# Two early loads of a retention-plus-MLP kernel, each issued as 120 + 8 partitions

## The chip, the cores and the metric

The kernel runs on one core of a Trainium2 chip. The metric is the device time of one launch in microseconds (us), as the median of three runs. One further execution was profiled; its span (first to last instruction) and its own device time are given below beside that median.

## The reference, cut to what matters

Two stages follow each other, all in fp32 in the reference. First a linear attention with decay in blocks of 64 rows, for 4 batches x 8 heads, 768 rows, head dimension 64. Then a two-layer MLP over all 3072 rows, 512 wide, 2048 hidden:

```python
intra = np.einsum('bhic,bhjc->bhij', qb, kb) * Dmask[None]
intra = np.einsum('bhij,bhjd->bhid', intra, vb)
inter = np.einsum('bhid,bhde->bhie', qb * lam_pow[None], kv_state)
out[:, :, sl] = intra + inter
kv_state = lam_block * kv_state + np.einsum('bhsd,bhse->bhde', kb_dec, vb)
...
h = x @ w_in
g = 0.5 * h * (1.0 + np.tanh(c * (h + 0.044715 * h * h * h)))
return (g @ w_out)
```

## The kernel before, in words

The attention is cut into 24 steps. A step is 256 rows of one batch and four of the eight heads; it loads q, k and v as tiles of 128 partitions, each partition with four heads x two neighbouring rows x 64 numbers (256 KB for each of the three). Two steps together give the attention output of 256 rows, transposed into `xT`, which is the input of the MLP. The MLP's rows are worked off in seven groups; group 0 holds the first 512 rows, so the output of steps 0 to 3. `queue_group` puts a group's work, in small pieces, into the list `filler`, and `fill(n)` takes the next n pieces out of it. The main part of the kernel, from line 930 on, is an order written out by hand: `prep` (casts), `stage_t` (transposes), `R`/`products`/`causal`/`update` (attention) and `fill` in between. Every instruction is pinned, so each engine runs its instructions in the order of the program, and what stands behind a waiting instruction waits too.

The first weights `moe_w_in` come as four blocks of 512 columns, j = 0 to 3, into fp32 staging tiles of 128 partitions x 4 chunks x 512, and are cast to fp16 on the chip. Blocks 0 and 1 come in two parts, of two chunks each (512 KB); blocks 2 and 3 in one piece (1 MB). The second weights `moe_w_out` come as four loads of 1 MB into the same staging tiles. All these loads are issued on SP, in this order: q, k and v of steps 0 to 2 (v of step 0 on ACT), q and k of step 3, the first part of block 0, v of step 3, the second part of block 0, the two parts of block 1, blocks 2 and 3, the four loads of `moe_w_out`, then q, k and v of steps 4 to 8. `lam`, the decay of each head, is an 8-partition load on ACT at the very start.

The loads that the change touches, and who reads them:

- v of step 3 is read by `scale_v(3)` on GpSimd (line 266). On TensorE, `products(3, None, banks)` (line 385) reads its result, behind `fill(8)`, the first eight pieces of group 0 (line 838, which use the first part of block 0).
- the second part of block 0 is read by the casts `cast_win(0, 0, 256, 128, c23, on_act=True)` on ACT (line 108) and `cast_win(0, 256, 512, 256, c23)` on VectorE (line 110). The next pieces, `fill(4)` (line 838), need them.

Later places that the prediction speaks of: block 2 of the first weights is cast at line 110 and first read by the matmuls of line 561. After `fill(9)` the order goes on with `prep(4); stage_t(4); prep(5); ... stage_t(5)`: q of steps 4 and 5 is scaled on VectorE (line 282), k of step 4 cast on VectorE (line 293) and k of step 5 on ACT (line 295), and `stage_t` transposes both on TensorE (line 321).

Of the kernel before, what the change touches and what calls it, by code (L numbers as in the profile page):

```python
# [15 lines left out]
def kernel(  # L16
# [10 lines left out]
    nc = tc.nc  # L27
    pin = tc.keep_in_program_order
    P = 128
# [25 lines left out]
    ps_M = ctx.enter_context(tc.tile_pool(name="psM", bufs=8, space=PSUM))  # L55


    ld32 = {}

    def load_step(s, names="qkv"):  # L60
        b, r = divmod(s, 2 * NSB)
        sb, half = divmod(r, 2)
        ts = ld32.setdefault(s, [])
        for nm, src in (("q", q), ("k", k), ("v", v)):
            if nm not in names:
                continue
            t = ld.tile([P, HH, 2, D], FP32, tag=nm + "32", name=f"{nm}32_{s}")
            rows = src[b, half * HH : (half + 1) * HH, sb * SB : (sb + 1) * SB, :]
            queue = nc.scalar if (nm, s) == ("v", 0) else nc.sync
            pin(queue.dma_start(out=t[:].rearrange("p h j d -> p h (j d)"),  # L70
                                in_=rows.rearrange("h (p j) d -> p h (j d)", j=2)))
            ts.append(t)

    w_in16 = w16p.tile([P, NC, DFF], FP16)
# [13 lines left out]
    def load_win(j, part=None):  # L88
        if not part:
            wstage[("i", j)] = wst.tile([P, NC, 512], FP32, tag=f"w{j}", name=f"wi32_{j}")  # L90
        t = wstage[("i", j)]
        src = moe_w_in[:, j * 512 : (j + 1) * 512].rearrange("(c p) f -> p c f", p=P)
        cs = slice(0, NC) if part is None else slice(2 * part, 2 * part + 2)
        pin(nc.sync.dma_start(out=t[:, cs, :], in_=src[:, cs, :]))

    def load_wout(j):
        t = wst.tile([P, 4, DM], FP32, tag=f"w{(0, 2, 1, 3)[j]}", name=f"wo32_{j}")
# [58 lines left out]
    for s in range(3):  # L156
        load_step(s)
    load_step(3, "qk")
    load_win(0, 0)
    load_step(3, "v")  # L160
    load_win(0, 1)
    for j in range(1, 4):
        for part in ((0, 1) if j < 2 else (None,)):
            load_win(j, part)
# [996 lines left out]
```

## Time and profile before

| | |
|---|---|
| median of 3 runs | 198.84 us (198.81 to 199.01) |
| the profiled execution | 198.79 us, span 197.0 us, so 1.8 us lie around the span |
| granted TensorE clock | 1.000 |
| TensorE matmuls busy | 191.2 us of the span |
| VectorE, ScalarE, GpSimd busy | 149.0, 121.1, 74.4 us |
| loaded from HBM, stored to it | 27.26 MB, 6.29 MB |
| first-weight loads of 512 KB, issue to landing (median) | 7.1 us |
| v loads of 256 KB, issue to landing (median) | 5.2 us |

In the views below a line of the timeline gives start and duration in us, the engine, the line of the kernel, the operation, output<-input, shape and count; brackets give the idle time of that engine just before and what ended it. PE is TensorE's matmuls, PEld its weight loads, DVE VectorE, ACT ScalarE, POOL GpSimd, and SPq the queue of SyncE that issues loads. In the chain of waits a line is start, duration and what held the end of the program back at that time.

### The profile page before, as it was taken

Reading aid. Unit: us, or ns where it says so; the run is one execution under the profiler, and the core shown is the slowest. Engines: PE = TensorE matmul, PEld = TensorE weight load, DVE = VectorE, ACT = ScalarE, POOL = GpSimd, SP = SyncE. Lnnn points to the kernel's source line nnn. Section 1 sums busy time; section 2 is a strip of 40 time slices with the busy share of each in tenths; the row PEclk is TensorE's granted clock in tenths of the full one; section 3 lists DMA queues with packets and bytes.
Section 4 is the critical chain, followed back from the end, with each engine's and each line's share of the span. In section 5 each row is a group of like instructions: output and inputs, shape, how many; then the busy total and the mean of one; then the engine's idle time right before and its main releaser. Section 6 shows DMA issues by size and latency. Waiting matters only on the chain.

```text
span 197.0 us, 5913 instructions
## 1 busy us (share of the span) xinstructions
PE 191.2 (97%) x2431; PEld 140.1 (71%) x2431; DVE 149.0 (76%) x291; ACT 121.1 (61%) x249; POOL 74.4 (38%) x85
## 2 busy tenths in 40 slices
PE   8979999999999999999999999999999999999993
PEld 2556544446888888654688764578888888888882
DVE  4797722889999889859999927999656987487620
ACT  3663878357874685686845378844867746679221
POOL 6594213457554931169754517165002030002000
PEclk9999999999999999999999999999999999999999
DMA  5999999999999999999996998400211300020205
GB/s 167 292 324 384 387 383 386 300 285 297 259 220 248 257 333 231 213 238 288 226 294 132 274 310 202 92 7 0 53 67 42 107 6 2 0 110 29 77 19 198
DMA packets 62810, 38.13 MB, mean 194 GB/s; under 512 B 18624, under 2 KB 55744, under 8 KB 62784
## 3 DMA queue, kind: packets, MB, share of 16 engines
q1 hardware_dynamic: 62240, 37.50, 74.3%
q8 instruction: 19, 0.31, 0.7%
q10 hardware_dynamic: 544, 0.26, 0.5%
q14 instruction: 7, 0.06, 0.1%
HBM read 27.26 MB, written 6.29 MB: 170 GB/s over the span
## 4 chain that ended last, share of the span: by engine, by line
PE 89%; SPq 4%; DMA 4%; ACT 0%; issue 0%
PE Hps L561 25%; PE MX L640 18%; PE MY L640 9%; PE HX L739 7%; PE O2ps L576 7%; PE MW L640 4%; DMA wi<-in_moe_w_in_dram 4%; SPq L70 4%; PE HY L739 4%; PE S L350 3%; PE Hps L838 3%; PE HW L739 2%; PE OK L408 2%; PE O L461 1%; PE O L436 1%; PE OK L399 1%
## 5 line engine op out<-in xcount | busy, mean ns | idle before, releaser
L561 PE MATMUL Hps<-xT,w_in 128*128 128x512 f16 (+1 forms) x288 | 50.5, 332 | 0.0
L513 POOL TENSOR_TENSOR u<-t,lumask 128x256 f16<-128x256 f32 x40 | 30.9, 788 | 40.7 <-DVE t L506 27.0
L561 PEld LDWEIGHTS <-w_in 128*128 128x128 f16 x288 | 27.9, 98 | 19.1
L565 ACT ACTIVATE gT<-Hps 128x512 f16<-128x512 f32 x56 | 33.5, 598 | 11.6 <-PE Hps L561 11.1
L360 DVE TENSOR_TENSOR PT<-S,mask 128x512 f16<-128x512 f32 x48 | 30.3, 680 | 7.8 <-PE S L350 7.8
L266 POOL TENSOR_TENSOR v<-v,dv 128x512 f16<-128x512 f32 x24 | 28.7, 1197 | 15.2 <-DMA v<-in_v_dram 14.0
L640 PEld LDWEIGHTS <-gs 128*128 128x128 f16 x320 | 31.2, 98 | 3.6
L640 PEld LDWEIGHTS <-gT 128*128 128x128 f16 x240 | 23.3, 98 | 3.2 <-ACT gT L565 0.2
L640 PE MATMUL MX<-w_sum,gs 128*128 128x256 f16 x160 | 21.4, 273 | 0.0
L692 POOL TENSOR_TENSOR o<-u,q 128x512 f32<-128x512 f32 (+1 forms) x5 | 6.3, 1252 | 36.7 <-ACT u L657 36.7
L282 DVE TENSOR_TENSOR qk<-q,dq 128x512 f16<-128x512 f32 x23 | 19.1, 833 | 0.8 <-DMA q<-in_q_dram 0.7
L295 ACT ACTIVATE qk<-k 128x512 f16<-128x512 f32 x23 | 14.4, 625 | 7.4 <-DMA k<-in_k_dram 7.3
L610 DVE TENSOR_TENSOR gs<-gT 128x1024 f16<-128x1024 f16 (+1 forms) x24 | 16.9, 711 | 1.6 <-ACT gT L565 1.6
L576 PE MATMUL O2ps<-w_out,gT 128*128 128x512 f16 x64 | 14.6, 379 | 0.0
L487 ACT ACTIVATE xT<-OK 128x256 f16<-128x256 f32 x26 | 9.9, 452 | 7.0 <-PE OK L408 6.5
L739 PEld LDWEIGHTS <-ws 128*128 128x128 f16 x128 | 12.5, 98 | 1.6 <-issue 0.2
L487 ACT ACTIVATE xT<-O 128x256 f16<-128x256 f32 x22 | 8.0, 461 | 5.8 <-PE O L461 4.9
L657 ACT ACTIVATE u<-MX 128x256 f32<-128x256 f32 x18 | 6.9, 384 | 7.4 <-PE MX L640 7.3
L576 PEld LDWEIGHTS <-gT 128*128 128x128 f16 x64 | 6.1, 98 | 6.6
L350 PEld LDWEIGHTS <-qkT 64*64 64x64 f16 x384 | 6.0, 106 | 6.8 <-issue 3.6
L640 PE MATMUL MY<-w_out,gs 128*128 128x256 f16 x80 | 10.7, 273 | 0.0
L753 DVE COPY u<-HX 128x512 f32<-128x512 f32 x8 | 5.5, 688 | 6.8 <-ACT gT L757 4.3
(98 smaller groups left out, 318.4 us busy)
## 6 DMA issues: line engine op xcount, KB each, us to landing
q<-in_q_dram SPq DMA_DIRECT2D x24, 256.0 KB, 4.9
k<-in_k_dram SPq DMA_DIRECT2D x24, 256.0 KB, 5.0
v<-in_v_dram SPq DMA_DIRECT2D x23, 256.0 KB, 5.2
out_dram<-o SPq DMA_DIRECT2D x23, 256.0 KB, 4.3
wo<-in_moe_w_out_dram SPq DMA_DIRECT2D x4, 1024.0 KB, 9.4
wi<-in_moe_w_in_dram SPq DMA_DIRECT2D x4, 512.0 KB, 7.1
wi<-in_moe_w_in_dram SPq DMA_DIRECT2D x2, 1024.0 KB, 12.5
v<-in_v_dram ACTq DMA_DIRECT2D x1, 256.0 KB, 4.3
```

What stands on the lines that cost most here:

```text
L266: pin(nc.gpsimd.tensor_tensor(wide(tv[:]), ld32[s][2][:], decay(dv, s), ALU.mult))
L282: pin(q_eng.tensor_tensor(wide(tq), q32[:], decay(dq, s), ALU.mult))
L295: pin(nc.scalar.activation(out=wide(tk), in_=k32[:], func=AF.Copy))
L360: pin(nc.vector.tensor_tensor(t[:, hl].rearrange("p b c d -> p b (c d)"), Sps[:].rearrange("p b c d -> p b (c d)"), mask[:].unsqueeze(1).t ...
L487: pin(nc.scalar.activation(out=d, in_=o, func=AF.Copy))
L513: pin(nc.gpsimd.tensor_tensor(u[:], state[half][:].unsqueeze(2).to_broadcast([P, 2, 2, D]), lumask[:, 2 * half : 2 * half + 2, :].unsqueez ...
L561: pin(nc.tensor.matmul(by_block(Hps[:, i, :]), w_in16[:, c, f * P : (f + 1) * P], x(c), start=(c == 0), stop=(c == NC - 1)))
L565: pin(nc.scalar.activation(out=dst, in_=Hps[:], func=AF.Gelu_apprx_tanh))
L576: pin(nc.tensor.matmul(O2[tau][0][:], gT[:, f % HF, f // HF, tau * P : (tau + 1) * P], w_out16[:, f, :], start=(n == 0), stop=(n == NF - 1)))
L610: pin(nc.vector.tensor_tensor(g_rows(m, i), g_rows(a, i), g_rows(b, i), op))
L640: pin(nc.tensor.matmul(dst, lhsT, rhs, start=(opens and i == 0), stop=(closes and i == HF - 1), skip_group_check=True))
L739: pin(nc.tensor.matmul(dst[:, i, :], w_in_block(a, slice(c, c + 1), slice(f * P, f * P + P))[:, 0], x_block(b, slice(c, c + 1))[:, 0], sta ...
```

## The change

The v load of step 3 and the load of the second part of block 0 are each issued as two transfers on SP: one of partitions 0 to 119 and one of partitions 120 to 127. The bytes, the tiles, the order of all loads and every reader stay. A reader now waits for two transfers. All other loads stay single.

```diff
+    even, uneven = (slice(0, P),), (slice(0, 120), slice(120, P))
     ld32 = {}
 
     def load_step(s, names="qkv"):
...
             queue = nc.scalar if (nm, s) == ("v", 0) else nc.sync
-            pin(queue.dma_start(out=t[:].rearrange("p h j d -> p h (j d)"),
-                                in_=rows.rearrange("h (p j) d -> p h (j d)", j=2)))
+            for ps in uneven if (nm, s) == ("v", 3) else even:
+                pin(queue.dma_start(out=t[ps].rearrange("p h j d -> p h (j d)"),
+                                    in_=rows.rearrange("h (p j) d -> p h (j d)", j=2)[ps]))
             ts.append(t)
...
         cs = slice(0, NC) if part is None else slice(2 * part, 2 * part + 2)
-        pin(nc.sync.dma_start(out=t[:, cs, :], in_=src[:, cs, :]))
+        for ps in uneven if (j, part) == (0, 1) else even:
+            pin(nc.sync.dma_start(out=t[ps, cs, :], in_=src[ps, cs, :]))
```

## The prediction

> **What bounds the kernel now.** I read the page first: which engine carries the time, whether the DMA queues are full, and how the chain that ended last is made up.
>
> ```profile
> PE 191.2 (97%) x2431; PEld 140.1 (71%) x2431; DVE 149.0 (76%) x291; ACT 121.1 (61%) x249; POOL 74.4 (38%) x85
> ...
> DMA  5999999999999999999996998400211300020205
> ...
> PE 89%; SPq 4%; DMA 4%; ACT 0%; issue 0%
> ```
>
> TensorE bounds the kernel, but each digit of the DMA row is 4.9 us, so up to about 100 us the 16 DMA queues are full as well. Both loads of the change lie in that time. The chain of waits from 0 to 35 us says where DMA holds the end:
>
> ```profile
> 9.35 0.47 SPq L70
> 9.81 0.04 issue
> 9.86 7.88 DMA wi<-in_moe_w_in_dram
> 17.74 0.02 issue
> 17.77 0.42 ACT w_in L108
> 18.19 0.05 issue
> 18.24 1.13 PE Hps L838 x8
> ```
>
> The load on this chain is the second part of block 0, issued at 9.86 and landed at 17.74. Everything behind it is TensorE. So I asked the timeline how long TensorE waits for it, and the DMA view of 13.5 to 15.5 us why it lands so late.
>
> ```profile
> 16.47 1.04 POOL L266 TENSOR_TENSOR v<-v,dv 128x512 f16<-128x512 f32 x1 [1.51 <-DMA v<-in_v_dram]
> ...
> 18.23 0.11 PEld L838 LDWEIGHTS <-w_in 128*128 128x128 f16 x2 [0.45 <-ACT w_in L108]
> 18.24 1.13 PE L838 MATMUL Hps<-xT,w_in 128*128 128x256 f16 x8 [0.35 <-ACT w_in L108]
> ...
> 18.54 0.55 PEld L838 LDWEIGHTS <-w_in 128*128 128x128 f16 x6 [0.19 <-ACT w_in L108]
> ```
>
> ```profile
> q8 instruction: 1, 0.02, 3.7%
> ```
>
> One instruction fetch of 16 KB sits between the loads there. The packet record has it at 13.81 us, 1.17 us long. The landing records hold one arrival for each queue of a transfer. The first part of block 0, before the fetch, has arrivals from 13.84 to 14.13 and the last at 14.32. For v of step 3 fifteen came by 15.11 and the sixteenth at 16.40; for the second part of block 0, by 16.46 and at 17.74. So one queue lost 1.3 us to the fetch and both readers wait for it. A second fetch starts at 20.08 (1.05 us), and block 2 has two late arrivals, 23.10 and 23.12, against 21.83 for the fourteenth: it fell on another queue. Call the first late queue X and the second Y.
>
> Last I asked what stands between 18 us and the end:
>
> ```profile
> 37.73 0.92 DVE L282 TENSOR_TENSOR qk<-q,dq 128x512 f16<-128x512 f32 x1 [0.53 <-DMA q<-in_q_dram]
> 38.64 0.43 DVE L293 CAST qk<-k 128x512 f16<-128x512 f32 x1
> 38.71 0.65 PEld L321 LDWEIGHTS <-qk 128*128 128x128 f16 x8
> ...
> 41.40 0.63 ACT L295 ACTIVATE qk<-k 128x512 f16<-128x512 f32 x1 [3.51 <-DMA k<-in_k_dram]
> ...
> 42.08 0.23 PEld L321 LDWEIGHTS <-qk 128*128 128x128 f16 x4 [0.20 <-ACT qk L295]
> ```
>
> This is the view that decides. The transposes of step 4 start 0.06 us after VectorE has scaled q, which waited for a load. Those of step 5 wait 0.20 us for ScalarE, which had waited 3.51 us for k of step 5 (landed at 41.32; the arrivals 41.29 and 41.32 I take for X and Y, the others came by 41.02). So at 42.08 TensorE is held by DMA again; in the waits from 43 to 110 us only GpSimd still waits for loads (9.4 us, three times), and the matmul row has no gap there.
>
> **The change part by part.** *What it removes.* 128 partitions give 16 arrivals, and `lam`, the one 8-partition load, gives eight; 120 does not divide by 16 but does by 15. I take 15 queues with 8 partitions each for the large transfer, 8 queues with one each for the small. Then one queue carries nothing of the two loads, eight carry 9 partitions and seven carry 8. If the idle queue is X, v lands near 15.1 and the weights near 16.5, each up to 0.35 later by what follows. TensorE then finds the cast done: 0.35 (matmul gap) + 0.19 (the weight load's second wait) = 0.54 us saved at 18.2 to 18.6. The other weight-load gap of 0.21 at 17.57 also stands at 19.30 with no wait behind it, so it is not counted. Nothing in the trace says which queue has the fetch; if X is another one, this saving is nothing.
>
> *What it adds on the queues.* Full transfers follow each other in 0.90 us for v (landings 0.90 apart) and 1.35 for a half block (17.74 to 19.10). One partition of eight more is 0.11 + 0.17 = 0.28 us on eight queues. Each extra transfer also costs a fixed bit: 32 packets of 27 ns are 0.86 of the 0.90, so about 0.04, twice: 0.07. Sum 0.35 us. These queues stay full beyond the loads of step 5, so this delay is carried on to each of them. It can't be below 0.28 if the split is 9 to 8. The readers' wait is now for the later of two landings, the small transfer's, since it stands behind the large one on the eight queues. Behind the waiting scale of v on GpSimd stand the u products of line 513, behind the cast on ScalarE the copies into xT (line 487), and TensorE waits for both; these 0.35 us are the price already counted, not a second one.
>
> *What it adds on SP.* Two more issues of 0.47 us (the rows of 10.68 to 11.70), 0.94 in all. Behind them on SP stand block 1's parts, blocks 2 and 3, then `moe_w_out`. The weights' second part is issued at 9.86, but its packets can't start before v's are through at about 15; the last of the row, block 3, is issued by 13.2 and starts after 21.5. The lead hides it: 0. Without it, up to 0.94.
>
> *Where the saving goes.* 0.54 us of lead at 18.6 reaches line 561 at 24.03, where block 2's first cast (23.14 + 0.43) leaves 0.46 of room: nearly all survives. At 38.71 it ends: q of step 4 lands at 37.71 whatever TensorE did, because Y is as late as X (37.70 and 37.71). At 42.08 it ends once more. So with X relieved the net is 41.32 - 41.29 = 0.03 us saved if Y is one of the seven, and 0.35 lost if Y is one of the eight, since q of step 4 and k of step 5 then land 0.35 later, and VectorE, ScalarE and TensorE wait for them in order. With X not relieved, it is 0.35 lost if X or Y is one of the eight. Eight of fifteen queues make the first chance 0.53; two draws out of fifteen make the second 1 - (7/15)(6/14) = 0.80. Most of the weight lies on +0.35: 198.79 + 0.35 = 199.14 for the profiled execution, and its median stands 0.05 higher: 199.2.
>
> [...]
>
> **The rivals.** *The 120-partition transfers run below full rate* (slower). No row shows a part transfer of any size. The mechanism is fewer queues or a shared path into the tile: were the large one to run on 8 queues, as `lam` does, each would carry 16 partitions instead of 8, so 0.90 + 1.35 = 2.25 us more. That lands on k of step 5 in full: 201.1. Half of that gives 200.0. It decides from 0.05 us over the 0.35 on. For it: 120 is no multiple of 16. Against it: queues work off packets one by one, 2 KB in 84 to 95 ns, which looks like each queue's own limit. [...]
>
> *The saving at 18.2 stays* (faster): 198.84 - 0.54 = 198.3. For it: this is the only gap in the matmul row after 13.3 us. Against it: 42.08, where k of step 5 would have to land 0.3 us earlier, with Y still late.
>
> *Nothing moves:* Y, and X if it is not relieved, are among the seven: 198.8.
>
> **How the numbers follow.** About 0.2% (0.4 us) is what a measurement of this kernel can tell from no change. Forecast, eight queues set the pace: chance 0.47, price 0.28 to 0.6 (the fixed bit may be larger than 0.04), so 0.29 within the line and 0.18 beyond it. Rate lost: 0.30, all slower. Nothing moves: 0.13. Saving stays: 0.10, faster. That is faster 0.10, same 0.42, slower 0.48. The range 198.6 to 200.4 holds the forecast (alone 199.1 to 199.5), the unmoved case and two thirds of the rate case; it leaves out the saving and the far end of the rate case, 0.2 together.
>
> **What would show it.** Right: the weight load's 0.45 and 0.19 at 18.2 are gone or not, as X is relieved or not; the wait of 0.20 at line 321 before k of step 5 grows to 0.5 or more with k landing near 41.65; after it the timeline is that of before, shifted. Rate lost: the fifteen early arrivals of v and of the weights move beyond 15.5 and 17.2. Wrong altogether: k of step 5 lands before 41.0 and the end moves up with it.

## The result, and the profile after

The changed kernel takes 202.02 us (median of 4 runs, 201.18 to 202.5) against 198.84 before: a ratio of 1.015, with an interval from 1.013 to 1.017. (Here and below a ratio is worked out from all runs of both kernels, so it can differ a little from the quotient of the two medians.) The forecast was 199.2 and its range ended at 200.4. The profiled execution took 202.5 us, span 200.7, at a mean granted clock of 0.991; before it was 198.79, 197.0 and 1.000. The page of after, read as the page of before was:

```profile
PE 192.4 (96%) x2431; PEld 140.9 (70%) x2431; DVE 150.2 (75%) x291; ACT 121.3 (60%) x249; POOL 74.3 (37%) x85
...
PEclk9999699999999999999999999999999999999999
DMA  6999999999989999999998999320202200021114
...
PE 88%; DMA 5%; SPq 4%; ACT 0%; issue 0%; ACTq 0%
```

TensorE is busy for 192.4 us instead of 191.2, with the same 2431 matmuls, and the clock row has a 6 in its fifth slice (20 to 25 us). DMA's share of the chain has grown from 4% to 5%. The DMA row shows next to nothing: the queues look as full as before. The chain of waits from the same stretch:

```profile
9.83 0.45 SPq L73
10.27 0.04 issue
10.32 9.44 DMA wi<-in_moe_w_in_dram
19.79 0.05 issue
19.84 0.43 ACT w_in L112
20.27 0.04 issue
20.31 1.89 PE Hps L842 x8
```

Two things differ. The load is 9.44 us on its way instead of 7.88 and is issued 0.46 us later, behind the second transfer of v; and the eight matmuls behind it take 1.89 us instead of 1.13. The windows (start:end and length, then each engine's busy time, and at the end granted clock, DMA share, GB/s) of the changed kernel show what lies behind both:

```profile
14.50:18.10 3.60, 3.20 (x52) 2.20 (x53) 2.64 (x8) 1.33 (x4) 1.07 (x2) 1.00 1.07 213
...
20.20:23.60 3.40, 3.29 (x30) 2.01 (x31) 1.96 (x5) 0.83 (x4) 1.36 (x2) 0.50 1.05 384
23.60:28.00 4.40, 4.40 (x26) 2.42 (x25) 3.02 (x8) 3.67 (x8) 0.73 (x1) 1.00 1.04 383
```

and the kernel before, for the stretch in which the same two loads move:

```profile
14.50:16.20 1.70, 1.70 (x43) 1.24 (x42) 1.70 (x8) 1.46 (x4) 0.46 (x1) 1.00 1.04 373
```

The share of busy queue time is 1.0 in both, but the queues move 213 GB/s in place of 373. The packet records say how: a packet of 2 KB takes 84 to 85 ns (median) in the second part of block 0 before, and 159 ns in the changed one. So here a full DMA row was no sign of a full rate. After 20.2 us, when only transfers of 128 partitions are left, the rate is 384 GB/s again. The second finding stands in the same lines: from 20.20 to 23.60 TensorE was granted 0.50 of its clock.

The timeline of the changed kernel around the two waits:

```profile
17.38 1.04 POOL L270 TENSOR_TENSOR v<-v,dv 128x512 f16<-128x512 f32 x1 [2.53 <-DMA v<-in_v_dram]
...
18.47 0.32 PE L389 MATMUL OK<-v,qk 64*64 64x64 f16 x16 [0.55 <-POOL v L270]
...
19.84 0.72 ACT L112 ACTIVATE w_in<-wi 128x256 f16<-128x256 f32 x2 [3.85 <-DMA wi<-in_moe_w_in_dram]
...
20.31 1.04 PE L842 MATMUL Hps<-xT,w_in 128*128 128x256 f16 x4 [1.52 <-ACT w_in L112]
```

A gap of 0.35 us before has become gaps of 0.55 and 1.52, after one of 0.22 at 16.66. The landing records, of the same two loads and of what follows (us):

| arrivals | before | after, large transfer | after, small transfer |
|---|---|---|---|
| v of step 3 | 14.69 to 15.11, last 16.40 | 15.08 to 15.91, last 17.31 | 15.39 to 15.99 |
| second part of block 0 | 16.05 to 16.46, last 17.74 | 17.66 to 18.15, last 19.75 | last 18.71 |
| block 1, last of each part | 19.10, 20.45 | 20.85, 22.21 | |
| q of step 4, k of step 5 | 37.71, 41.32 | 39.59, 43.19 | |

The loads behind are 1.75 to 2.0 us late, all of them up to step 5. But TensorE is later still. Its landmarks (us): the matmuls that wait for the weights start at 18.24 before and 20.31 after (+2.07); those of block 2 at 24.25 and 27.68 (+3.43, so 1.36 more in the stretch at half clock); the transposes of step 4 at 38.92 and 42.36; the last matmul ends at 193.72 and 196.95 (+3.23); the span ends 3.29 us after that before, and 3.77 after (+0.48). Those last two make the 3.71 us of the two spans.

### The profile page after: what moved, and what is told of

It is laid out like the page before. It is cut to its first block, busy times and chain, and to the rows that moved or that the text cites. A ratio compares the mean times of both kernels' runs of the same rounds, so it can differ in the third digit from the quotient of the medians.

```text
span 200.7 us, 5919 instructions
## 1 busy us (share of the span) xinstructions
PE 192.4 (96%) x2431; PEld 140.9 (70%) x2431; DVE 150.2 (75%) x291; ACT 121.3 (60%) x249; POOL 74.3 (37%) x85
## 4 chain that ended last, share of the span: by engine, by line
PE 88%; DMA 5%; SPq 4%; ACT 0%; issue 0%; ACTq 0%
PE Hps L565 24%; PE MX L644 17%; PE MY L644 9%; PE HX L743 7%; PE O2ps L580 7%; DMA wi<-in_moe_w_in_dram 5%; PE MW L644 4%; SPq L73 4%; PE HY L743 3%; PE Hps L842 3%; PE S L354 3%; PE HW L743 2%; PE OK L412 2%; PE OK L403 1%; PE O L465 1%; PE O L440 1%
## 5 line engine op out<-in xcount | busy, mean ns | idle before, releaser
L517 POOL TENSOR_TENSOR u<-t,lumask 128x256 f16<-128x256 f32 x40 | 31.4, 799 | 44.6 <-DVE t L510 30.5
L696 POOL TENSOR_TENSOR o<-u,q 128x512 f32<-128x512 f32 (+1 forms) x5 | 5.7, 1145 | 36.6 <-ACT u L661 36.6
```

The source lines that it names most:

```text
L517: pin(nc.gpsimd.tensor_tensor(u[:], state[half][:].unsqueeze(2).to_broadcast([P, 2, 2, D]), lumask[:, 2 * half : 2 * half + 2, :].unsqueez ...
```

## The experiments

**Does a transfer of fewer partitions lose rate?** The question was put first to a kernel that only loads: the kernel's computation is left out, and one shape of transfer follows the other on SP, six times each. `two_kb` loads two rows of 2 KB to a partition, as the second part of block 0; the two phases with `rows` in their name load four of 512 B, as v.

```diff
+    def split_120_8():
+        for i in range(6):
+            t = slot(f"b{i}")
+            two_kb(t, slice(0, 120))
+            two_kb(t, slice(120, P))
...
+    for phase in (whole_128, split_120_8, only_120, split_112_16, halves_64, only_64,
+                  rows_128, rows_120_8, whole_128_again):
+        phase()
```

> Only loads, back to back on SP; no attention and no MLP is computed, and one 128-row tile is stored. Theory 1 (a part transfer runs at a lower rate as long as it lasts): transfers over 128 partitions move about 385 GB/s as in the timeline of before, those over 120 about 220 to 260, with the small 8-partition transfer adding little; 64 partitions, although they divide by 16, are slow as well, about 220. Theory 2 (every further transfer has a fixed price): 120 partitions alone move about 360 GB/s (15 of 16 queues), 64 + 64 and 112 + 16 are as slow as 120 + 8. Theory 3 (a count of partitions that isn't a power of two is slow to issue): 64 partitions run at the full rate, 112 and 120 don't.

The windows of this run, for 128 partitions, 120 + 8, 120 alone, 112 + 16, the lower and the upper 64 in turn, and the lower 64 alone:

```profile
4.50:11.80 7.30, 0.00 (x0) 0.00 (x0) 1.00 1.05 383
16.90:27.30 10.40, 0.00 (x0) 0.00 (x0) 1.00 1.00 215
29.40:41.00 11.60, 0.00 (x0) 0.00 (x0) 1.00 1.04 225
42.90:50.60 7.70, 0.00 (x0) 0.00 (x0) 1.00 1.05 268
54.30:66.60 12.30, 0.00 (x0) 0.00 (x0) 1.00 1.07 234
...
67.80:74.00 6.20, 0.00 (x0) 0.00 (x0) 1.00 1.11 213
```

The share of busy queue time is 1.0 or more in every line, and the rate falls to between 56% and 70%. By the spacing of the landings: 512 KB take 1.35 us as 128 partitions, 2.45 on average (2.1 to 2.6) as 120 + 8, 1.93 as 112 + 16; 480 KB of 120 partitions alone take 2.3, which is 214 GB/s (its window shows 225, because the sixteenth queue, which has no part in these loads, already moves data of the next phase). The lower and the upper 64 partitions in turn take 1.12 us each for 256 KB, the lower 64 again and again 1.25, which is 210 GB/s. With rows of 512 B, 256 KB take 0.88 at full width and 1.09 on average (1.0 to 1.2) as 120 + 8. The loss is that of the narrow transfer itself: 120 partitions lose it without the small one. And 64 and 112 lose it too, though they divide by 16 and data arrive from all 16 queues, so neither the number of queues nor the divisor decides. Theory 1 stood, with 120 alone a little below its 220 GB/s; the price for this change is 1.1 us for the weights and 0.2 for v.

**Each half alone.** In the changed kernel only v, or only the weights, keeps its two transfers:

```diff
-        for ps in uneven if (j, part) == (0, 1) else even:
+        for ps in even:
```

> Only v of step 3 is split 120 + 8. Theory 1: its fifteen early arrivals come about 0.4 us later than before, every later load too, and the kernel takes 0.4 to 0.8 us more: 199.2 to 199.6. Theory 2: half of the whole change's loss, about 1.6 us: 200.4.

```diff
-            for ps in uneven if (nm, s) == ("v", 3) else even:
+            for ps in even:
```

> Only the second part of block 0 is split 120 + 8. Theory 1: it lands about 1.2 to 1.3 us later than before, 19.0, and the kernel takes 1.3 to 2.5 us more, above 200.1. Theory 2: half of the loss, 200.4, as for v alone.

v alone: 199.42 us, ratio 1.0028 (1.0016 to 1.0039). The v arrivals come 0.45 to 0.8 us later, the weights' last at 18.34 instead of 17.74. Weights alone: 200.56, ratio 1.009 (1.0057 to 1.0124), last arrival 19.32. In the kernel the narrow transfers thus cost more than where loads run alone: 0.6 and 1.58 us at the weights' landing against 0.2 and 1.1. In the second kernel v, which is whole again, is complete at 16.85 instead of 16.40, so a narrow transfer seems to slow its neighbour too; the rest of the difference is not explained. The sum of the two over their common 198.85 is 0.57 + 1.71 = 2.28 us; both together had cost 3.2. The waits of TensorE in the second kernel (us in all, times, longest):

```profile
PEld L842 <- ACT w_in L112: 1.8, 2, 1.6
...
PE Hps L842 <- ACT w_in L112: 1.5, 1, 1.5
```

The wait is nearly as long as in the changed kernel (1.5 there as well), yet the clock after it was not cut:

```profile
20.00:23.40 3.40, 3.40 (x41) 2.27 (x40) 2.56 (x7) 1.45 (x5) 1.81 (x3) 1.00 1.05 387
```

In 3.4 us there are 41 matmul records here and 30 in the changed kernel. One of this kernel's four executions, at a mean clock of 0.991, took 201.63 us, the other three 200.47 to 200.58. So the missing 0.9 us was looked for in the clock. (A second measurement of the changed kernel, below, puts it 2.47 us over the kernel before, and then only 0.2 us are missing: most of the 0.9 lies in how many executions lose clock.)

**The same number of transfers at full width.** v is split by heads (3 + 1), the weights by chunks (1 + 1), each transfer over all 128 partitions:

```diff
+            for hs in ((slice(0, 3), slice(3, 4)) if (nm, s) == ("v", 3) else (slice(0, HH),)):
+                pin(queue.dma_start(out=t[:, hs].rearrange("p h j d -> p h (j d)"),
+                                    in_=rows.rearrange("h (p j) d -> p h (j d)", j=2)[:, hs]))
...
+        for c in ((slice(2, 3), slice(3, 4)) if (j, part) == (0, 1) else (cs,)):
+            pin(nc.sync.dma_start(out=t[:, c, :], in_=src[:, c, :]))
```

> Both loads are again two transfers each, but each over all 128 partitions: v by heads (3 and 1), the weights by chunks (1 and 1). Theory 1: no loss of rate, landings within 0.15 us of before, 198.7 to 199.1. Theory 2: the same number of transfers as in the change, so most of its loss: above 200.5.

199.24 us, ratio 1.0012 (1.0001 to 1.0022), 0.14 us above what theory 1 gave. Both transfers of v are complete at 16.65, those of the weights at 17.91, the first part of block 1 at 19.27: 0.17 to 0.25 us later than before, where the change costs 0.9 to 2.0. So it is the width that counted here and not the number of transfers. The last matmul ends only 0.09 us later; but the time from there to the end of the span is 3.78 us, as in the changed kernel, against 3.29. That was not expected and is taken up below.

**Is the rest the clock?** Three zero matmuls are put into the longest gap, on an open accumulation (`firsts` keeps hold of its bank), so that TensorE has work while it waits; the loads stay those of the change. Beside it the changed kernel was run once more.

```diff
+    firsts = []
...
         first = {}
+        if g == 0:
+            firsts.append(first)
...
     causal(3)
+    zero = nc.const_aps.tensor(0.0, (P, P), FP32)
+    for _ in range(3):
+        pin(nc.tensor.matmul(firsts[0][0][:, 0:256], zero, ones[FP32][:, 0:256],
+                             start=False, stop=False, skip_group_check=True))
     cast_win(0, 0, 256, 128, c23, on_act=True)
```

> The changed kernel, with three matmuls of zeros (256 wide, fp32) added into an open bank behind the products of v of step 3, so that TensorE works where it waits for the second part of block 0. Theory A (the 0.7 us and more that the two part losses do not explain come from the lower granted clock after the wait): granted clock 1.0 in every execution, times within 0.4 us of each other, 201.0 to 201.4. Theory B (they come from the two part losses adding up on the queues): 201.2 to 202.5 as before.

> The changed kernel unaltered, as a companion for the others: 201.2 to 202.5, the longer times in executions with a granted clock below 1.0.

The changed kernel again took 201.41 us (201.15 to 203.37), ratio 1.0153 (1.0099 to 1.0208). Its profiled execution, 201.15 us, had a gap of 1.59 us in the same place, and no half clock behind it; the one with the lowest mean clock, 0.992, took 203.37. With the zero matmuls the four runs lie within 0.12 us: 201.34 to 201.46, ratio 1.012 (1.0105 to 1.0135), mean clock 0.998 or more. So the half clock goes with the spread of the changed kernel's times. With TensorE kept busy it did not occur, which four executions do not prove, since five of the eight of the changed kernel have none either; what the last section says of the clock rests on the traces. What remains without it is 2.46 us over 198.94. The median is no better than that of the changed kernel in the same set, 201.40 against 201.41. In this kernel TensorE comes early enough to be held by the late loads of steps 4 and 5 (q of step 4 lands at 39.79), which in the first profile of the changed kernel it was not. Its weight-load waits from 14 to 45 us:

```profile
PEld L325 <- DVE qk L286: 0.3, 1, 0.3
...
PEld L325 <- ACT qk L299: 0.2, 1, 0.2
```

**Another width.** 112 + 16 partitions in place of 120 + 8:

```diff
-    even, uneven = (slice(0, P),), (slice(0, 120), slice(120, P))
+    even, uneven = (slice(0, P),), (slice(0, 112), slice(112, P))
```

> Both loads split 112 + 16: all 16 queues carry as many partitions as in one load of 128. Theory 1 (the queues of a part transfer share paths into the tile; the rate run gave 270 GB/s for 112 + 16 against 205 for 120 + 8): the second part of block 0 lands 0.6 to 0.9 us later than before and the kernel takes 199.6 to 200.4. Theory 2 (15 queues and the late one among them make the loss): no loss, 198.7 to 199.1.

200.47 us, ratio 1.008 (1.0045 to 1.0114). The theory without a loss is out. The size is 0.07 above what theory 1 gave, but it came about in another way: the bulk of v's arrivals is hardly late (14.73 to 15.07), while the last of the large transfer comes at 17.11 and of the small one at 17.38; the weights' bulk ends at 16.82, their last arrivals come at 19.11 and, of the small transfer, 19.28. The delay here stands mostly on the queue that was late already; why is not shown. The profiled execution again had 3.4 us at half clock, behind gaps of 1.14 and 0.85 us:

```profile
19.80:23.20 3.40, 3.40 (x30) 2.07 (x31) 1.71 (x4) 0.82 (x3) 1.36 (x2) 0.50 1.05 384
```

**A late landing without any narrow transfer.** All loads at full width and single, but the first part of block 1 is issued ahead of the second part of block 0:

```diff
     load_step(3, "v")
+    load_win(1, 0)
     load_win(0, 1)
-    for j in range(1, 4):
-        for part in ((0, 1) if j < 2 else (None,)):
-            load_win(j, part)
+    load_win(1, 1)
+    for j in range(2, 4):
+        load_win(j)
```

> The kernel before, all loads full width, with the first part of block 1 ahead of the second part of block 0, so that this one lands 1.35 us later and every load behind the two as before. Theory A (the loss runs through the landing of this one load and TensorE's order behind it): 1.2 to 1.6 us more, 200.0 to 200.4, and up to 1 us on top where the clock falls. Theory B (it runs through the loads of steps 4 and 5, which every later load's delay reaches): less than 0.4 us more.

199.84 us, ratio 1.0041 (1.0026 to 1.0057). In the profiled execution the weights land at 19.11 (+1.37), TensorE waits 1.28 us, and the last matmul ends 1.17 later, though the loads of steps 4 and 5 land as before (37.68 and 41.28). By the medians the loss is 0.90 us, 0.16 below theory A's range; theory B, that the loss runs through the later loads alone, is out. So a late landing here costs two thirds of its delay or more, and little of it is made good behind it on TensorE.

**Which widths, and two queues at once.** Loads alone again: two halves of 64 at once, one issued on SP and one on ACT, then 96, 32, 16 and 8 partitions (`few(n, k)` loads the first n partitions k times).

```diff
+            for ps, queue in ((lo, nc.sync), (hi, nc.scalar)):
...
+                pin(queue.dma_start(out=t[:].rearrange("p (c f) -> p c f", c=2)[ps],
+                                    in_=src[ps, 2 * part : 2 * part + 2, :]))
...
+    few(96, 4)
+    few(32, 6)
+    few(16, 6)
+    few(8, 6)
```

> Only loads again, and one 128-row tile stored. First 64 partitions on SP and the other 64 on ACT at the same time, then on SP alone 128, 96, 32, 16 and 8 partitions. [...] Theory 1b (every queue is slower in a transfer that isn't 128 partitions wide): both halves at once 234 in all, and 32 and 16 partitions, which also divide by 16, 234 each; 8 partitions half of that.

By the spacing of the landings: 96 partitions 1.40 us for 384 KB (281 GB/s), 32 0.67 us for 128 KB (196), 16 0.60 us for 64 KB (109), 8 0.61 us for 32 KB (54). Theory 1b, which gave 234 for 32 and for 16 and half of that for 8, is too high in all three. In the last two a transfer has only two packets on a queue, and 16 and 8 partitions take the same 0.6 us, so a fixed time for each transfer would give these two as well. The two halves on two queues fill the first fifteen slices of the run, of 1.26 us each:

```profile
GB/s 0 26 297 229 237 245 303 305 294 289 248 232 232 230 230 333 388 386 388 386 386 347 277 282 281 286 214 208 206 128 107 58 57 107 141 381 237 0 208 0
```

In eight slices they move 229 to 248 GB/s, about what one half after the other moved (234), and in five 289 to 305; the sixteen halves land 1.02 us apart on average, 257 GB/s. Theory 1b asked for 234 in all, so it does not hold as it stands here either. The rate goes with the width of a transfer, and what sets it is not shown. A packet of 2 KB takes 84 to 88 ns at 128 partitions, 122 at 96, 171 at 32 and 304 at 16 and 8.

**The longer end.** Two more variants of the kernel split by heads and chunks: one with a further SP issue (an 8-partition load of `lam` that nobody reads), one with the two stores of pair 0 issued on ACT, which takes two issues from SP.

```diff
+    pin(nc.sync.dma_start(out=lam_more[:], in_=lam.unsqueeze(1)))
```

> The kernel with both loads split along the free dimension, and one more issue on SP: a load of lam into a tile that nothing reads. In that split kernel 0.45 us of its loss lies behind TensorE's last matmul. Theory E (the end of SP's program waits for a fetch of its own code, and where that falls depends on the number of instructions on SP): with one more issue the stretch from the last matmul to the end is 3.3 us again, and the time 198.8 to 199.0. Theory F (each further transfer costs by itself): 199.3 or more.

```diff
+            queue = nc.scalar if pair == 0 else nc.sync
-            pin(nc.sync.dma_start(out=rows[:, i], in_=o_pairs[pair][:, i]))
+            pin(queue.dma_start(out=rows[:, i], in_=o_pairs[pair][:, i]))
```

> The kernel with both loads split along the free dimension, with the two stores of the first pair of output tiles (at about 57 us) issued on ACT instead of SP: as many transfers as in the split kernel, but only as many issues on SP as in the kernel before. Theory E' (the 0.45 us behind TensorE's last matmul come with the number of instructions on SP): that stretch is 3.3 us again, and the time 198.8 to 199.0. Theory F (they come with the number of transfers): it stays 3.7 to 3.8 us, 199.2 or more.

One more: 199.30 us, ratio 1.0033 (1.0008 to 1.0057), end stretch 3.72 us: a further issue adds nothing. Two fewer on SP: 199.12, ratio 1.0028 (1.0009 to 1.0048); the end stretch is 3.37, near that of before, but the last matmul ends 0.2 us later than in the split kernel, so the time as a whole hardly moves. The kernels with one issue more than before (v alone 3.33, weights alone 3.39) have the short end as well. So the end is about 0.45 us longer from two SP issues more on, whatever they load (3.72 to 3.78 us in every profile with two or three more, 3.28 to 3.39 in those with none or one). SyncE's last six instructions, up to the end of the span, take 1.4 us in the long ends and 0.8 to 1.0 in the short ones; why is not shown.

## Why the prediction was wrong

**What bounds the kernel** was read rightly: TensorE, held by the second part of block 0 near 18 us. That the DMA queues are full up to about 100 us was read from their busy share, which did not tell their rate: at a share of 1.0 they moved 373 GB/s before and 213 in the changed kernel.

**The queue counts.** Right: the large transfer has one arrival at once (9.92, 10.83) and fifteen with data, the small one eight.

**The saving at 18.2.** It did not come. The small transfers are complete at 15.99 and 18.71, and the late arrivals, 17.31 and 19.75, are of the large ones: X is one of the seven queues that carry 8 partitions. This also turns round the sentence on which landing the reader waits for: it is the large transfer's. The 0.54 us were counted too high as well: the eight matmuls with the second wait of 0.19 take 1.13 us, and eight without it 1.05 (line 842 at 15.61 in the changed kernel), so only about 0.08 of it was to be had.

**The price on the queues, 0.28 + 0.07 = 0.35 us: this is the term that failed.** It took 120 partitions at the full rate of 128. It measured 0.91 us at the last arrival of v (16.40 to 17.31) and 2.01 at that of the weights (17.74 to 19.75), and the loads behind them are 1.75 to 2.0 late. The rival "rate lost" was the mechanism, with up to 2.25 us and a chance of 0.30, but the reason given for it, eight queues in place of sixteen, was wrong: fifteen carry the data and each packet takes longer (159 ns in place of 84 to 85). The argument against it, that a packet's 84 to 95 ns look like each queue's own limit, fell with the 159 ns. The fixed cost of a further transfer was small, as forecast, but more than 0.07: at full width two more of them move the landings by 0.17 to 0.25 us. No run shows the 9-to-8 share of 0.28 by itself.

Sharing the queues is not what costs: the transfers split by heads and chunks share them too, and landed at most 0.25 us late. The loss went with the width: of the widths that were run only 128 partitions reached 386 GB/s, while the lower 64 alone moved 210 and the lower 32 moved 196.

**Two more SP issues at 0.** Right for the loads: the DMA share stays at 1.04 or more from 20.2 to 28 us, where their packets move. Wrong at the end of the program, where two more issues went with 0.48 us.

**Where it goes.** The prediction let the price end at k of step 5, with a wait of 0.5 us or more at the transposes. In the changed kernel there is none; the timeline around them:

```profile
40.57 0.68 DVE L286 TENSOR_TENSOR qk<-q,dq 128x512 f16<-128x512 f32 x1
...
42.14 0.65 PEld L325 LDWEIGHTS <-qk 128*128 128x128 f16 x8
...
43.27 0.63 ACT L299 ACTIVATE qk<-k 128x512 f16<-128x512 f32 x1 [3.49 <-DMA k<-in_k_dram]
```

No bracket stands at line 286 nor at 325: TensorE was already 3.4 us late and the loads 1.9, so it never met them. In this execution the loss had fallen at 18 to 24 us; the kernel that delays one landing alone shows that such a loss stays. In the second profile of the changed kernel, without the half clock, TensorE is 1.92 us late at the weights, and VectorE waits 0.57 us for q of step 4 (39.68, before 37.71), as it waited 0.53 before. There both places cost the same 1.9 us, once and not twice, and the forecast's place was one of them.

**What was not priced at all** is the clock: 1.36 us in the profiled execution. The five executions of the two runs at a mean clock of 0.999 or more took 201.15 to 201.76, so the rate and the end stretch alone leave the range; the clock takes it to 202 and beyond. The kernel before can lose clock as well: of its executions in all these sets one had a mean clock of 0.991 and took 199.77.

The signs that it named for a lost rate, fifteen early arrivals beyond 15.5 and 17.2, came for the weights clearly (17.66 to 18.15), for v hardly: 13 of its 15 arrivals came by 15.44, and only the last early one, at 15.91, beyond 15.5. The bill for the profiled execution, in us of the span: wait at 18 to 20 +2.07, half clock +1.36, taken back later -0.20, end +0.48; in all 3.71. By parts, v alone 0.57, weights alone 1.71 and the end 0.45 add up to 2.73; the kernel with zero matmuls, which has all three and no half clock, measured 2.46, so the parts do not simply add up: some 0.3 us of them count once. Which is not shown.

## What to carry to other kernels

A load that covers 128 partitions should not be cut by partitions: cut it along the free dimension if it must be cut, since that moved the landings by 0.25 us at most, while 8 partitions less made each packet nearly twice as long (159 ns in place of 84 to 85). A busy share of 1.0 did not tell the rate of the DMA queues, which moved 373 GB/s at it and 213; look at the GB/s and at a packet's duration. And a price at a load on which TensorE waits should carry the clock with it: in the kernels whose waits near 18 us added up to 1.8 to 2.3 us, 5 of 18 executions lost 1 to 2 us more to it.

## What the runs showed of the hardware that was not expected

The rate of loads from HBM into one partition range, one transfer after another: 128 partitions 386 GB/s, 96 281, 120 alone 214, the lower 64 210 (lower and upper 64 in turn 234), 32 196, 16 109, 8 54. It does not rise evenly with the width: 120 partitions are slower than 96 and hardly faster than 64. Why is open.

TensorE ran at half clock for 3.4 us behind gaps of 0.22, 0.55 and 1.52 us in one execution (and of 1.14 and 0.85 in the kernel with 112 + 16), and at full clock behind 0.30, 0.34 and 1.59 in another of the same kernel. The clock records of the traces show what differs. The records of the granted clock begin or change, in the changed kernel, at 6.53, 20.18, 23.59 and 201.09 us, with 112 + 16 at 6.11, 19.76, 23.17 and 200.67, and in the kernel before at 6.91 and 198.06. The half clock lasts 3.413 us, and the other distances are 4, 52 and 56 times that; where the points fall in the program differs from one execution to the next. In the 3.41 us before the fall TensorE was busy for 1.36 us and, with 112 + 16, for 1.43. If such points also lie where the clock stays as it is, which no record shows, one of them, at 19.46 in the second profile of the changed kernel, lies inside the longest gap; the gaps are then shared out to two stretches with 1.89 and 2.71 us of work, and the clock stayed. With the weights alone the emptier stretch has 2.00. So the clock fell behind 1.36 and 1.43 us of work in 3.41 and stayed behind 1.89 and more; that the work in such a stretch is what decides is the author's reading, and two falls are few.
